# Gated two-branch decode attention in fp32: units of one head against units of four heads in three 8 MB tiles

## The chip, the core and the metric

The kernel runs on one core of one Trainium2 chip. The metric is the device time of one execution, in microseconds, smaller is better. The core has a matrix engine (PE, "TensorE") that multiplies from SBUF into PSUM, a vector engine (DVE), a scalar engine (ACT), GpSimd (POOL), a sync engine (SP) that here only issues transfers, and 16 DMA engines that carry every transfer between HBM and SBUF.

## What is computed

One decode step for two batch rows. Two attention branches A and B read the same `x`, each with its own query weights, key cache, value cache and output weights; a sigmoid gate mixes them. Everything is fp32.

```python
B, Sq, D = 2, 1, 512;  Hq, Sk, Dh = 32, 4096, 128
q = (x @ wq).reshape(B, Sq, Hq, Dh).transpose(0, 2, 1, 3)
scores = einsum("bhqd,bhkd->bhqk", q, k_cache) * Dh ** -0.5
o = einsum("bhqk,bhkd->bhqd", softmax(scores, axis=-1), v_cache)
branch = o.transpose(0, 2, 1, 3).reshape(B, Sq, Hq * Dh) @ wo
g = sigmoid((x * gate_w).sum(-1, keepdims=True))
out = g * branch_A + (1 - g) * branch_B
```

Each key or value cache is 2 x 32 heads x 4096 tokens x 128 floats, 134 MB, and there are four of them; each of the four weight matrices is 8 MB. Every byte is read once, 570 MB in all, and there is one query per head, so a byte of a cache is used for one multiply and one add.

## The kernel before

**Units.** The work is cut into 128 units, one head of one batch row of one branch each (`units`, L44), in the order branch, head, batch row. The 4096 tokens of a head lie on 128 partitions, 32 tokens to a partition, so a unit's K tile and its V tile are 128 x 4096 floats, 2 MB each, and a partition receives one run of 16 KB. There are four K buffers and five V buffers.

**A unit on the engines.** DVE multiplies the K tile in place by the query, which lies on all partitions (L141), sums over the 128 dimensions (L145), and takes the largest score per partition (L147). PE transposes that column (L151), DVE takes the maximum over partitions (L155), and ACT exponentiates, writing the weights into a zero-padded tile of 32 columns and the sums into `lp` (L158). PE multiplies the weights with V in eight matmuls, each of them in one of four strips of 32 array columns (L165); ACT copies the result to SBUF (L169); PE gathers one head's output (L177) and the sum of the exponentials over partitions (L184). DVE inverts that sum and normalises (L188, L192), and PE adds the head's share of the output projection (L197).

**What sets the order.** The schedule is manual: each engine executes its instructions in the order of the code. The main loop (L228) is a software pipeline: in the round of unit u it computes the scores of u, the softmax of u - 1 and the values of u - 2, and it normalises the pair of heads that is finished with u - 3. So DVE's `invert` and `normalise` stand one round or more behind the PE work that they read.

**Loads.** One list, `todo` (L208), sets the order of all loads on SP's queue: K two units ahead of V, a 2 MB piece of the query weights for each group of eight heads (`load_wq`, L69), and 1 MB of output weights for every four heads (`load_wo`, L75). SP waits at a load until the buffer it writes is free, and everything behind it in the list waits too. The small loads of `x` and of the gate weights come first (L82, L83). The query weights of the next group are projected between the units (`project`, L109), and the queries are copied from PSUM to SBUF by ACT (L119).

**The end.** The last V tile comes in four pieces (L65); after the last of them there follow the rest of that unit's values matmuls, ACT's copy, the gather, the normalisation, the output projection, the gated sum (L203) and the store (L205).

Of the kernel before, what the change touches and what calls it, by code (L numbers as in the profile page):

```python
# [13 lines left out]
P = 128  # L14
B = 2
# [4 lines left out]
NS = SK // P  # L20
KC = D // P
HG = 8
OG = 4
VC = 4
NVC = NS // VC
NPR = 3
QT = 32
STRIPS = P // QT
LEAD = 2
# [4 lines left out]
def tile_gated_decode(ctx: ExitStack, tc: tile.TileContext, ins: dict, out: bass.AP):  # L34
    nc = tc.nc
    consts = ctx.enter_context(tc.tile_pool(name="consts", bufs=1))
    kpool = ctx.enter_context(tc.tile_pool(name="kpool", bufs=4))
    vpool = ctx.enter_context(tc.tile_pool(name="vpool", bufs=5))
    wpool = ctx.enter_context(tc.tile_pool(name="wpool", bufs=2))
    work = ctx.enter_context(tc.tile_pool(name="work", bufs=3))  # L40
# [3 lines left out]
    units = [(n, h, b) for n in "AB" for h in range(H) for b in range(B)]  # L44
    NU = len(units)
    groups = [(n, g) for n in "AB" for g in range(H // HG)]
    per_group = HG * B

    kt, vt, wq, wo, qs = {}, {}, {}, {}, {}

    def tokens(cache, h, b):

        return cache[b, h].rearrange("(p r) d -> p r d", p=P)

    def load_k(u):
        n, h, b = units[u]
        kt[u] = kpool.tile([P, NS, DH], F32, name="kt")
        nc.sync.dma_start(kt[u], tokens(ins[n + "_k_cache"], h, b))

    def load_v(u):  # L60
        n, h, b = units[u]
        vt[u] = vpool.tile([P, NS, DH], F32, name="vt")
        src = tokens(ins[n + "_v_cache"], h, b)

        cuts = (0, NS) if u < NU - 1 else (0, NS // 2, 3 * NS // 4, NS - VC, NS)  # L65
        for i, j in zip(cuts, cuts[1:]):
            nc.sync.dma_start(vt[u][:, i:j], src[:, i:j])

    def load_wq(g):  # L69
        n, hg = groups[g]  # L70
        wq[g] = wpool.tile([P, KC, HG * DH], F32, name="wq", bufs=1)
        nc.sync.dma_start(
            wq[g], ins[n + "_wq"].rearrange("(c p) f -> p c f", p=P)[:, :, hg * HG * DH:(hg + 1) * HG * DH])

    def load_wo(n, hg):  # L75
        wo[n, hg] = wpool.tile([P, OG, D], F32, name="wo", bufs=2)
        nc.sync.dma_start(
            wo[n, hg], ins[n + "_wo"].rearrange("(h p) e -> p h e", p=P)[:, hg * OG:(hg + 1) * OG, :])


    rows = consts.tile([B * KC + KC, P], F32)
    nc.sync.dma_start(rows[:B * KC], ins["A_x"].rearrange("b s (c p) -> (b s c) p", p=P))  # L82
    nc.scalar.dma_start(rows[B * KC:], ins["gate_w"].rearrange("(c p) -> c p", p=P))  # L83
    load_wq(0)
# [4 lines left out]
    ones = consts.tile([P, P], F32)  # L89
    nc.vector.memset(ones, 1.0)  # L90


    padded = []
    for i in range(NPR):
        t = consts.tile([P, NVC, QT], F32, name=f"pr{i}")
        nc.vector.memset(t, 0.0)
        padded.append(t)

    pick = consts.tile([P, VC], F32)
    nc.vector.tensor_reduce(pick, ident.rearrange("p (s q) -> p q s", q=QT)[:, :VC, :], axis=AX.X, op=ALU.add)  # L100

    cols_ps = ps.tile([P, B * KC + KC], F32, name="mt", bufs=1)
    nc.tensor.transpose(cols_ps, rows, ident[:B * KC + KC, :B * KC + KC])
    cols = consts.tile([P, B * KC + KC], F32)
    nc.vector.tensor_copy(cols, cols_ps)
    xb = consts.tile([P, B * KC, P], F32)
    nc.vector.tensor_copy(xb, cols[:, :B * KC, None].to_broadcast([P, B * KC, P]))

    def project(g, i):  # L109

        b, half, c = i // (2 * KC), i // KC % 2, i % KC
        if i % (2 * KC) == 0:
            qs[g, b] = work.tile([P, HG * DH], F32, name=f"q{b}", bufs=2)
        if c == 0:
            qp[g] = ps.tile([P, HG * DH // 2], F32, name="qp", bufs=2)
        cols = slice(half * HG * DH // 2, (half + 1) * HG * DH // 2)
        nc.tensor.matmul(qp[g], xb[:, b * KC + c, :], wq[g][:, c, cols], start=c == 0, stop=c == KC - 1)  # L117
        if c == KC - 1:
            nc.scalar.activation(qs[g, b][:, cols], qp[g], AF.Copy, scale=SCALE)  # L119

    qp = {}
    for i in range(per_group):
        project(0, i)


    z = ps.tile([B, 1], F32, name="small", bufs=1)
    for c in range(KC):
        nc.tensor.matmul(z, cols[:, c:B * KC:KC], cols[:, B * KC + c:B * KC + c + 1],
                         start=c == 0, stop=c == KC - 1)
    gate = consts.tile([B, 4], F32)  # L130
    nc.scalar.activation(gate[:, 0:1], z, AF.Exp, scale=-1.0)  # L131
    nc.vector.tensor_scalar(gate[:, 1:2], gate[:, 0:1], 1.0, None, op0=ALU.add)  # L132
    nc.vector.reciprocal(gate[:, 2:3], gate[:, 1:2])
    nc.vector.tensor_scalar(gate[:, 3:4], gate[:, 2:3], -1.0, 1.0, op0=ALU.mult, op1=ALU.add)

    sc, rm, mt, pr, lp, vp, ot, ls, acc, part, vs, on, rs = ({} for _ in range(13))

    def scores_mult(u):
        n, h, b = units[u]
        q = qs[groups.index((n, h // HG)), b][:, (h % HG) * DH:(h % HG + 1) * DH]  # L140
        nc.vector.tensor_tensor(kt[u], kt[u], q[:, None, :].to_broadcast([P, NS, DH]), op=ALU.mult)  # L141

    def scores_sum(u):
        sc[u] = work.tile([P, NS], F32, name="sc")
        nc.vector.tensor_reduce(sc[u], kt[u], axis=AX.X, op=ALU.add)  # L145
        rm[u] = work.tile([P, 1], F32, name="rm")
        nc.vector.tensor_reduce(rm[u], sc[u], axis=AX.X, op=ALU.max)  # L147

    def spread_max(u):
        mt[u] = ps.tile([P, P], F32, name="mt", bufs=1)  # L150
        nc.tensor.transpose(mt[u], rm[u].to_broadcast([P, P]), ident)  # L151

    def soft(u):
        nm = work.tile([P, 1], F32, name="nm")
        nc.vector.tensor_reduce(nm, mt[u], axis=AX.X, op=ALU.max, negate=True)  # L155
        pr[u] = padded[u % NPR]
        lp[u] = work.tile([P, 1], F32, name="lp", bufs=4)
        nc.scalar.activation(pr[u][:, :, :VC], sc[u].rearrange("p (c a) -> p c a", a=VC), AF.Exp,  # L158
                             bias=nm, accum_out=lp[u])

    def values(u):
        vp[u] = ps.tile([P, VC * DH], F32, name="vp", bufs=2)
        for c in range(NVC):
            s = c % STRIPS
            nc.tensor.matmul(vp[u][s * QT:(s + 1) * QT], pr[u][:, c, :],  # L165
                             vt[u][:, c * VC:(c + 1) * VC, :].rearrange("p a d -> p (a d)"),
                             start=c < STRIPS, stop=c >= NVC - STRIPS)
        vs[u] = work.tile([P, VC * DH], F32, name="vs", bufs=1)
        nc.scalar.activation(vs[u], vp[u], AF.Copy)  # L169

    def gather_out(u):
        n, h, b = units[u]
        if b == 0:
            ot[n, h] = ps.tile([P, B], F32, name="ot", bufs=1)
        o = ot[n, h]
        for a in range(VC):
            nc.tensor.matmul(o[:, b:b + 1], vs[u][:, a * DH:(a + 1) * DH], pick[:, a:a + 1],  # L177
                             start=a == 0, stop=a == VC - 1)

    def sum_of(u):  # L180
        n, h, b = units[u]
        if b == 0:
            ls[n, h] = ps.tile([P, B], F32, name="small", bufs=1)
        nc.tensor.matmul(ls[n, h][:, b:b + 1], ones, lp[u], start=True, stop=True)  # L184

    def invert(n, h):
        rs[n, h] = work.tile([P, B], F32, name="rs")
        nc.vector.reciprocal(rs[n, h], ls[n, h])  # L188

    def normalise(n, h):  # L190
        on[n, h] = work.tile([P, B], F32, name="on")
        nc.vector.tensor_tensor(on[n, h], ot[n, h], rs[n, h], op=ALU.mult)  # L192

    def project_out(n, h):
        if h == 0:
            acc[n] = ps.tile([B, D], F32, name="acc", bufs=1)
        nc.tensor.matmul(acc[n], on[n, h], wo[n, h // OG][:, h % OG, :], start=h == 0, stop=h == H - 1)  # L197
        if h == H - 1:
            part[n] = consts.tile([B, D], F32, name="part" + n)
            if n == "A":  # L200
                nc.vector.tensor_scalar(part[n], acc[n], gate[:, 2:3], None, op0=ALU.mult)  # L201
            else:
                nc.vector.scalar_tensor_tensor(part[n], acc[n], gate[:, 3:4], part["A"],  # L203
                                               op0=ALU.mult, op1=ALU.add)
                nc.sync.dma_start(out.rearrange("b s e -> (b s) e"), part[n])  # L205


    todo = []  # L208
    for u in range(-LEAD, NU):
# [3 lines left out]
        if u < 0:  # L213
            continue
# [63 lines left out]
```

## Time and profile before

| | |
|---|---|
| median of 3 runs | 1349.0 us (1348.57 to 1349.04) |
| the profiled execution's own span, first to last instruction | 1344.6 us |
| median less that span | 4.4 us |
| bytes read from HBM | 570.43 MB |
| mean granted TensorE clock | 0.714 |
| DVE busy / PE busy / ACT busy | 1181.0 / 819.0 / 149.0 us |
| K loads, V loads | 128 and 128 of 2 MB (the last V in four pieces) |

A page of the profile shows how long each engine was busy, the span in 40 equal slices, the DMA queues, the chain of work that ended last, and the groups of instructions. L141 is line 141 of the kernel. PE is busy with matmuls, PEld with weight loads; an fp32 matmul appears as two records. A queue's packets are its transfers' runs: a row of 16 KB that goes to one partition is one packet of one DMA engine. "Landing" is the moment at which a transfer's completion is seen.

### The profile page before, as it was taken

Reading aid. Unit: us, or ns where it says so; the run is one execution under the profiler, and the core shown is the slowest. Engines: PE = TensorE matmul, PEld = TensorE weight load, DVE = VectorE, ACT = ScalarE, POOL = GpSimd, SP = SyncE. Lnnn points to the kernel's source line nnn. Section 1 sums busy time; section 2 is a strip of 40 time slices with the busy share of each in tenths; the row PEclk is TensorE's granted clock in tenths of the full one; section 3 lists DMA queues with packets and bytes.
Section 4 is the critical chain, followed back from the end, with each engine's and each line's share of the span. In section 5 each row is a group of like instructions: output and inputs, shape, how many; then the busy total and the mean of one; then the engine's idle time right before and its main releaser. Section 6 shows DMA issues by size and latency. Waiting matters only on the chain.

```text
span 1344.6 us, 9688 instructions
## 1 busy us (share of the span) xinstructions
PE 819.0 (61%) x3849; PEld 326.5 (24%) x3849; DVE 1181.0 (88%) x652; ACT 149.0 (11%) x418; POOL 0.7 (0%) x6
## 2 busy tenths in 40 slices
PE   5468755657545675466754666557665466655566
PEld 2223322322212222122212223122222122222222
DVE  2999997989889898898988989889898898989985
ACT  1011110111100111011100111101110011110111
POOL 0000000000000000000000000000000000000000
PEclk9568776688666876678866678656786677866667
DMA  9999999999999999999999999999999999999996
GB/s 390 429 434 428 430 429 429 432 429 429 430 430 432 429 429 428 429 431 431 430 429 428 429 431 432 427 431 427 432 432 427 432 429 429 431 428 432 428 431 266
DMA packets 50041, 571.07 MB, mean 425 GB/s; under 512 B 4542, under 2 KB 4554, under 8 KB 17228
## 3 DMA queue, kind: packets, MB, share of 16 engines
q1 hardware_dynamic: 49988, 570.45, 99.6%
q8 instruction: 30, 0.49, 0.1%
q14 instruction: 15, 0.12, 0.0%
q10 hardware_dynamic: 8, 0.00, 0.0%
HBM read 570.43 MB, written 0.00 MB: 424 GB/s over the span
## 4 chain that ended last, share of the span: by engine, by line
DMA 68%; DVE 27%; PE 2%; issue 2%; ACT 0%; SPq 0%; ACTq 0%
DMA kt<-in_B_k_cache_dram 36%; DMA kt<-in_A_k_cache_dram 27%; DVE sc L145 14%; DVE kt L141 12%; DMA vt<-in_B_v_cache_dram 3%; DMA vt<-in_A_v_cache_dram 2%; PE qp L117 1%; PE vp L165 1%; DMA wq<-in_A_wq_dram 1%; PE acc L197 0%; DVE nm L155 0%; DVE rm L147 0%; PE ot L177 0%; DVE on L192 0%; DVE partA L201 0%
## 5 line engine op out<-in xcount | busy, mean ns | idle before, releaser
L165 PE MATMUL vp<-vt,pr 128*32 128x512 f32 x2048 | 417.9, 961 | 422.1 <-DMA vt<-in_B_v_cache_dram 237.3
L141 DVE TENSOR_TENSOR kt<-kt,q 128x4096 f32<-128x4096 f32 x128 | 566.1, 4422 | 117.7 <-DMA kt<-in_B_k_cache_dram 65.1
L145 DVE TENSOR_REDUCE sc<-kt 128x32 f32<-128x4096 f32 x128 | 564.2, 4408 | 0.3 <-DVE nm L155 0.3
L165 PEld LDWEIGHTS vp<-vt,pr 128*32 128x32 f32 x2048 | 71.5, 147 | 578.9 <-DMA vt<-in_B_v_cache_dram 242.6
L177 PEld LDWEIGHTS ot<-pick,vs 128*128 128x128 f32 x1024 | 149.8, 223 | 13.9 <-issue 10.2
L177 PE MATMUL ot<-pick,vs 128*128 128x1 f32 x1024 | 141.2, 259 | 0.8 <-ACT vs L169 0.8
L117 PE MATMUL qp<-wq,xb 128*128 128x512 f32 x256 | 133.6, 651 | 6.3 <-DMA wq<-in_A_wq_dram 6.3
L169 ACT ACTIVATE vs<-vp 128x512 f32<-128x512 f32 x128 | 76.3, 596 | 443.8 <-PE vp L165 443.8
L158 ACT ACTIVATE pr<-sc,nm 128x32 f32<-128x32 f32 x128 | 41.1, 321 | 688.4 <-DVE nm L155 688.4
L151 PE MATMUL mt<-ident,rm 128*128 128x128 f32 x128 | 44.2, 345 | 90.8 <-DVE rm L147 90.6
L197 PE MATMUL acc<-wo,on 128*2 128x512 f32 x128 | 95.6, 841 | 0.3 <-DVE on L192 0.3
L117 PEld LDWEIGHTS qp<-wq,xb 128*128 128x128 f32 x256 | 48.3, 208 | 112.2 <-issue 112.2
L151 PEld LDWEIGHTS mt<-ident,rm 128*128 128x128 f32 x128 | 18.7, 146 | 222.5 <-DVE rm L147 193.5
L184 PE MATMUL small<-lp,ones 128*128 128x1 f32 x256 | 51.5, 271 | 0.0
L184 PEld LDWEIGHTS small<-lp,ones 128*128 128x128 f32 x256 | 45.3, 221 | 0.0
L155 DVE TENSOR_REDUCE nm<-mt 128x1 f32<-128x128 f32 x128 | 36.2, 283 | 0.3 <-PE mt L151 0.3
L197 PEld LDWEIGHTS acc<-wo,on 128*2 128x2 f32 x128 | 15.4, 122 | 83.7 <-issue 75.4
L147 DVE TENSOR_REDUCE rm<-sc 128x1 f32<-128x32 f32 x128 | 23.8, 186 | 4.4
L119 ACT ACTIVATE q<-qp 128x512 f32<-128x512 f32 x32 | 19.1, 597 | 56.8 <-PE qp L117 56.8
L158 ACT ACTIVATION_READ_ACCUMULATOR pr<-sc,nm 128x1 f32 x128 | 23.9, 187 | 0.0
L132 DVE TENSOR_SCALAR gate<-gate 2x1 f32<-2x1 f32 x1 | 0.1, 142 | 22.9 <-ACT gate L131 22.9
L188 DVE RECIPROCAL rs<-small 128x2 f32<-128x2 f32 x64 | 10.2, 160 | 5.6 <-PE small L184 5.6
(22 smaller groups left out, 16.6 us busy)
## 6 DMA issues: line engine op xcount, KB each, us to landing
kt<-in_A_k_cache_dram SPq DMA_DIRECT2D x64, 2048.0 KB, 30.0
vt<-in_A_v_cache_dram SPq DMA_DIRECT2D x64, 2048.0 KB, 34.4
kt<-in_B_k_cache_dram SPq DMA_DIRECT2D x64, 2048.0 KB, 32.4
vt<-in_B_v_cache_dram SPq DMA_DIRECT2D x63, 2048.0 KB, 35.5
wq<-in_A_wq_dram SPq DMA_DIRECT2D x4, 2048.0 KB, 14.4
wo<-in_A_wo_dram SPq DMA_DIRECT2D x8, 1024.0 KB, 31.9
wq<-in_B_wq_dram SPq DMA_DIRECT2D x4, 2048.0 KB, 34.0
wo<-in_B_wo_dram SPq DMA_DIRECT2D x8, 1024.0 KB, 32.0
```

Source lines behind the costliest of these rows:

```text
L117: nc.tensor.matmul(qp[g], xb[:, b * KC + c, :], wq[g][:, c, cols], start=c == 0, stop=c == KC - 1)
L141: nc.vector.tensor_tensor(kt[u], kt[u], q[:, None, :].to_broadcast([P, NS, DH]), op=ALU.mult)
L145: nc.vector.tensor_reduce(sc[u], kt[u], axis=AX.X, op=ALU.add)
L147: nc.vector.tensor_reduce(rm[u], sc[u], axis=AX.X, op=ALU.max)
L151: nc.tensor.transpose(mt[u], rm[u].to_broadcast([P, P]), ident)
L155: nc.vector.tensor_reduce(nm, mt[u], axis=AX.X, op=ALU.max, negate=True)
L158: nc.scalar.activation(pr[u][:, :, :VC], sc[u].rearrange("p (c a) -> p c a", a=VC), AF.Exp, bias=nm, accum_out=lp[u])
L165: nc.tensor.matmul(vp[u][s * QT:(s + 1) * QT], pr[u][:, c, :], vt[u][:, c * VC:(c + 1) * VC, :].rearrange("p a d -> p (a d)"), start=c < S ...
L169: nc.scalar.activation(vs[u], vp[u], AF.Copy)
L177: nc.tensor.matmul(o[:, b:b + 1], vs[u][:, a * DH:(a + 1) * DH], pick[:, a:a + 1], start=a == 0, stop=a == VC - 1)
L184: nc.tensor.matmul(ls[n, h][:, b:b + 1], ones, lp[u], start=True, stop=True)
L197: nc.tensor.matmul(acc[n], on[n, h], wo[n, h // OG][:, h % OG, :], start=h == 0, stop=h == H - 1)
```

## The change

**Units of four heads.** A unit is now four heads of one batch row (`HU` = 4), 32 units in the order branch, batch row, group of four heads. Each head takes 32 partitions and a partition holds 128 tokens (`SLOTS`). A K or V tile is 128 x 16384 floats, 8 MB, and a partition receives one run of 64 KB. A pad of 96 floats in front brings the tiles' SBUF addresses to multiples of 512 bytes. There are two buffers named `kt` and one named `vt`, and nothing else of that size: the query weights of a branch (8 MB in one load) and B's output weights take a `kt` buffer, A's output weights the `vt` buffer, and the last V tile a `kt` buffer.

**Scores.** The multiply reads the query from PSUM: the projection of a branch writes four PSUM tiles `q`, in strips, where the 32 partitions of each head hold that head's query, and they stay there. The maximum per head is found by a 32 x 32 transpose on DVE and no longer by PE. Four exponentials per unit, one for each head's 32 partitions, write one padded tile `pr`, and their sums go into a column per head of `lsum`.

**Values.** 32 matmuls per unit; an even and the following odd unit add into one PSUM tile, which ACT copies after the odd one; one matmul with `strip` puts the pair into its 32 rows of `gat`. After the last group of a batch row (`g == HG - 1`, units 7, 15, 23 and 31) `outputs` picks, sums, normalises and gates the 32 heads at once.

**No software pipeline.** The loop does scores, softmax and values of the same unit in one round; `outputs` stands in the round of its last unit. The loads stand in the loop: after softmax u comes the load of K u + 2, after values u that of V u + 1. In rounds 14 and 15 B's query weights and the first two K tiles of B come in.

**Output weights last.** Both branches' output weights are loaded after the last V tile, B's in six pieces, and the whole output projection follows the loop. The gate is applied in `outputs`, so that A and B add into one PSUM tile.

**Small loads.** `x` and the gate weights now come in three loads on ACT's queue, 128 rows of 16 bytes each. SP's first load is A's query weights. `z`, the gate's sum, is one matmul that stands on PE ahead of the projection and needs all three of them.

```diff
-    units = [(n, h, b) for n in "AB" for h in range(H) for b in range(B)]
+    units = [(n, b, g) for n in "AB" for b in range(B) for g in range(HG)]
...
+    def cache(name, u):
+        n, b, g = units[u]
+        c = ins[f"{n}_{name}_cache"][b, g * HU:(g + 1) * HU]
+        return c.rearrange("h (s t) d -> (h s) t d", t=SLOTS)
...
+    def load_wq(n):
+        wq[n] = big.tile([P, KC, H * DH], F32, name="kt")
+        nc.sync.dma_start(wq[n], ins[n + "_wq"].rearrange("(p c) f -> p c f", c=KC))
...
+    load_wq("A")
+    xg = consts.tile([P, B + 1, KC], F32)
+    for b in range(B):
+        nc.scalar.dma_start(xg[:, b], ins["A_x"][b, 0].rearrange("(p c) -> p c", c=KC))
+    nc.scalar.dma_start(xg[:, B], ins["gate_w"].rearrange("(p c) -> p c", c=KC))
+    load_k(0)
...
+    z = ps.tile([H, B], F32, name="small")
+    nc.tensor.matmul(z, ones, zp, start=True, stop=True)
...
+    def project(n):
+        for b in range(B):
+            for half in range(2):
+                q = ps.tile([P, HG // 2, DH], F32, name="q", bufs=4)
...
+                for c in range(KC):
+                    for h in range(HU):
+                        nc.tensor.matmul(
+                            q[h * QP:(h + 1) * QP], xb[:, b, c, :],
+                            cols[:, c, h, half * HG // 2:(half + 1) * HG // 2, :],
+                            start=c == 0, stop=c == KC - 1)
...
+    def scores(u):
+        n, b, g = units[u]
+        q = qs[n, b, g // (HG // 2)][:, g % (HG // 2), :]
+        nc.vector.tensor_tensor(kt[u], kt[u], q[:, None, :].to_broadcast([P, SLOTS, DH]), op=ALU.mult)
+        sc[u] = work.tile([P, SLOTS], F32, name="sc")
+        nc.vector.tensor_reduce(sc[u], kt[u], axis=AX.X, op=ALU.add)
...
+        if odd:
+            vs = work.tile([P, VC * DH], F32, name="vs", bufs=1)
+            nc.scalar.activation(vs, o, AF.Copy)
...
+            nc.tensor.matmul(gat[n, b][r:r + QP], strip, vs, start=True, stop=True)
+            if g == HG - 1:
+                outputs(n, b)
+
+    def outputs(n, b):
+        gs = work.tile([P, VC, DH], F32, name="vs", bufs=1)
+        nc.scalar.activation(gs, gat[n, b].rearrange("p (a d) -> p a d", a=VC), AF.Copy)
+        lt = ps.tile([H, 1], F32, name="small")
+        nc.tensor.matmul(lt, lsum, ones[:, 0:1], start=True, stop=True)
+        rl = work.tile([H, 2], F32, name="rl")
+        nc.vector.reciprocal(rl[:, 0:1], lt)
+        nc.vector.tensor_tensor(rl[:, 1:2], rl[:, 0:1], gate[:, 2 + (n == "B"), b:b + 1], op=ALU.mult)
...
+    project("A")
+    load_k(1)
+    load_v(0)
+    for u in range(NU):
+        scores(u)
+        soft(u)
+        if u == per_branch - 2:
+            load_wq("B")
+        elif u == NU - 2:
+            load_v(NU - 1)
+        elif u == NU - 1:
+            load_wo("B")
+        else:
+            load_k(u + 2 if u != per_branch - 1 else per_branch)
+            if u == per_branch - 1:
+                project("B")
+                load_k(per_branch + 1)
+        values(u)
+        if u == NU - 2:
+            load_wo("A")
+        elif u < NU - 2:
+            load_v(u + 1)
```

Three places where the order of instructions differs. First DVE in the middle of a branch, before: `kt` is a K tile, `small` the PSUM tile of the sums, `rs` its reciprocal, `ot` and `on` a head's output.

```order
L145 TENSOR_REDUCE sc_1386<-kt_1270 128x32
L147 TENSOR_REDUCE rm_1388<-sc_1386 128x1
L188 RECIPROCAL rs_1402<-small_1356 128x2
L141 TENSOR_TENSOR kt_1306<-kt_1306,q0_995 128x4096
L155 TENSOR_REDUCE nm_1415<-mt_1404 128x1
L192 TENSOR_TENSOR on_1419<-ot_1372,rs_1402 128x2
L145 TENSOR_REDUCE sc_1421<-kt_1306 128x32
```

And DVE now, from the scores of unit 7, the last of its batch row, to those of unit 8: `rl` is the reciprocal of the sums `small`.

```order
L147 TENSOR_TENSOR kt_452<-kt_452,q_129 128x16384
L149 TENSOR_REDUCE sc_542<-kt_452 128x128
L154 TENSOR_REDUCE rm_544<-sc_542 128x1
L156 STREAM_TRANSPOSE tm_546<-rm_544 128x32
L158 TENSOR_REDUCE nm_548<-tm_546 128x1
L193 RECIPROCAL rl_595<-small_593 32x1
L194 TENSOR_TENSOR rl_595<-rl_595,gate_107 32x1
L147 TENSOR_TENSOR kt_504<-kt_504,q_146 128x16384
```

The reciprocal before read the sums of a unit that PE had in an earlier round; now it reads the sums of the unit that DVE has just scored, and the multiply of the next unit stands behind it.

Next the first instructions of SP's queue, before (`rows` is the tile of `x`):

```order
L82 DMA rows<-in_A_x_dram 8x128
L72 DMA wq<-in_A_wq_dram 128x4x1024
L58 DMA kt<-in_A_k_cache_dram 128x4096 x3
L77 DMA wo<-in_A_wo_dram 128x4x512
L67 DMA vt<-in_A_v_cache_dram 128x4096
```

and now, where `kt` is the buffer that holds the query weights, then K tiles:

```order
L72 DMA kt<-in_A_wq_dram 128x16384
L61 DMA kt<-in_A_k_cache_dram 128x16384 x2
L68 DMA vt<-in_A_v_cache_dram 128x16384
L61 DMA kt<-in_A_k_cache_dram 128x16384
L68 DMA vt<-in_A_v_cache_dram 128x16384
```

`x` is gone from SP's queue, and the second K tile goes into the buffer of the query weights. Last the start of ACT's queue now; `xg` holds `x` and the gate weights:

```order
L87 DMA xg<-in_A_x_dram 128x4 x2
L88 DMA xg<-in_gate_w_dram 128x4
L121 ACT_TABLE_LOAD
L121 ACTIVATE gate<-small 32x2
L162 ACTIVATE pr,lsum<-sc,nm 32x32x4 x8
```

Before there was one load there, the gate weights in four rows of 512 bytes.

More of the change, by code (lines that the diff above doesn't have):

```diff
@@ L186, in invert @@
[L186 to L205, printed above, removed]
```

275 lines of the change are left out of this document (120 added, 155 removed).

## The prediction

> **What bounds the kernel now.** I read the page first: the slices, then the chain.
>
> ```profile
> span 1344.6 us, 9688 instructions
> ...
> PE 819.0 (61%) x3849; PEld 326.5 (24%) x3849; DVE 1181.0 (88%) x652; ACT 149.0 (11%) x418; POOL 0.7 (0%) x6
> ...
> GB/s 390 429 434 428 430 429 429 432 429 429 430 430 432 429 429 428 429 431 431 430 429 428 429 431 432 427 431 427 432 432 427 432 429 429 431 428 432 428 431 266
> ...
> HBM read 570.43 MB, written 0.00 MB: 424 GB/s over the span
> ...
> DMA 68%; DVE 27%; PE 2%; issue 2%; ACT 0%; SPq 0%; ACTq 0%
> ```
>
> The row of GB/s is flat from the second slice to the last but one, the chain is mostly K loads, and no engine is busy all the time (DVE 88%). So the transfers set the time. The stretch between the ends, and two stretches of it with the runs sorted by size, say how fast they go (the last columns of the first row are granted clock, DMA share, GB/s):
>
> ```profile
> 20.00:1320.00 1300.00, 792.00 (x3739) 314.92 (x3738) 1168.41 (x635) 143.86 (x408) 0.00 (x0) 0.71 1.01 430
> ```
>
> ```profile
> DMA packets 1249, 18.12 MB, mean 431 GB/s; under 512 B 143, under 2 KB 143, under 8 KB 143
> ```
>
> ```profile
> DMA packets 463, 1.89 MB, mean 421 GB/s; under 512 B 1, under 2 KB 1, under 8 KB 463
> ```
>
> The first stretch moves 430 GB/s, and 570.43 MB at that rate are 1326.6 us of a span of 1344.6 us. The second (62 to 104 us) holds K and V runs of 16 KB only, the third (44.9 to 49.4 us) the query weights' runs of 4 KB. Only three things can change the time: the rate, holes in the stream of transfers, and what lies ahead of the first and behind the last.
>
> **Rate.** At 431 GB/s a run of 16 KB takes one of 16 DMA engines 16384 x 16 / 431 = 608 ns; at 421 one of 4 KB takes 155.7 ns. The difference, 452 ns for 12288 bytes, is 36.8 ns per KB of 1000 bytes; what is left of a run is 4.9 ns of its own. A 64 KB run comes to 4.9 + 2413 = 2418 ns, or 433.7 GB/s. Nothing of before moves a 64 KB run, so the bounds are 430 (no gain) and 434; I take 433, near the extrapolation, since nearly all bytes now come in such runs. 570.43 / 0.433 = 1317.4 us, 9.2 us less than now; at 430 it is 1326.6, at 434 1314.4. An 8 MB tile takes 19.4 us.
>
> One rule speaks against the longer runs. The Trainium skill, DMA: Bandwidth & Descriptors, section Latency and other measured facts, lists transfers whose 128 rows lie a large power of two apart in HBM: 207 GB/s at 512 KiB against 214 at full rate, 164 at 2 MiB. Here the pitch goes from 16 to 64 KiB, which it does not list, and no run here shows it; if the 3% of 512 KiB held, an estimate by that page is 41 us more. I give it no more than 2 in 100.
>
> **Compute beside it.** These rows carry the price of a unit of four heads:
>
> ```profile
> L141 DVE TENSOR_TENSOR kt<-kt,q 128x4096 f32<-128x4096 f32 x128 | 566.1, 4422 | 117.7 <-DMA kt<-in_B_k_cache_dram 65.1
> L145 DVE TENSOR_REDUCE sc<-kt 128x32 f32<-128x4096 f32 x128 | 564.2, 4408 | 0.3 <-DVE nm L155 0.3
> ...
> L155 DVE TENSOR_REDUCE nm<-mt 128x1 f32<-128x128 f32 x128 | 36.2, 283 | 0.3 <-PE mt L151 0.3
> ...
> L147 DVE TENSOR_REDUCE rm<-sc 128x1 f32<-128x32 f32 x128 | 23.8, 186 | 4.4
> ```
>
> The multiply and the sum over a tile four times as large cost at most 4 x 4422 = 17.7 us each; if up to 186 ns of each (the 32-element row L147) is a fixed part, at least 17.1. I take 17.25, so 34.5 us for both. That the multiply now reads its query from PSUM I price at nothing (L155 reads 128 elements from PSUM in 283 ns, L147 32 from SBUF in 186: 1 ns per element either way); 0.5 us a unit is the other bound. With the small maximum steps (under 1 us) DVE needs about 35.4 us per unit, the transfers 38.7. So DVE stays under cover, by 3 us per unit. For PE:
>
> ```profile
> 8.93 16.80 PE L117 MATMUL qp<-wq,xb 128*128 128x512 f32 x32 [6.28 <-DMA wq<-in_A_wq_dram]
> ...
> 14.18 0.34 PEld L117 LDWEIGHTS qp<-wq,xb 128*128 128x128 f32 x1 [0.52 <-issue]
> 14.84 0.19 PEld L117 LDWEIGHTS qp<-wq,xb 128*128 128x128 f32 x1 [0.32 <-issue]
> ...
> 45.71 3.42 PE L165 MATMUL vp<-vt,pr 128*32 128x512 f32 x16
> ```
>
> The first row is a dense burst that starts cold: the weight loads take 0.34 us until 14.18 and 0.19 us from 14.84 on, when the clock doubles, some 5.6 us after the start. The last row is one unit's eight strip matmuls at half clock, 0.43 us each. At the end of the span they run at full clock:
>
> ```profile
> 1336.57 1.92 PE L165 MATMUL vp<-vt,pr 128*32 128x512 f32 x16
> ...
> 1337.02 0.13 PEld L165 LDWEIGHTS vp<-vt,pr 128*32 128x32 f32 x4 [0.30 <-issue]
> 1337.45 0.13 PEld L165 LDWEIGHTS vp<-vt,pr 128*32 128x32 f32 x4 [0.30 <-issue]
> 1338.67 0.60 ACT L169 ACTIVATE vs<-vp 128x512 f32<-128x512 f32 x1 [4.39 <-PE vp L165]
> ...
> 1339.32 1.05 PE L177 MATMUL ot<-pick,vs 128*128 128x1 f32 x8 [0.83 <-ACT vs L169]
> 1340.41 0.16 DVE L192 TENSOR_TENSOR on<-ot,rs 128x2 f32<-128x2 f32 x1 [3.57 <-PE ot L177]
> ...
> 1341.68 0.74 DVE L203 SCALAR_TENSOR_TENSOR partB<-acc,gate,partA 2x512 f32<-2x512 f32 x1 [1.11 <-PE acc L197]
> 1342.45 0.27 SPq L205 DMA_DIRECT2D out_dram<-partB  x1
> ```
>
> Four weight loads (two matmuls) per 0.43 us are 0.215 us per matmul. The 32 values matmuls of a unit follow over 25 us of idle PE: 5.6 us cold (13 of them), 19 warm at 0.215, with the last one's drain 9.9 us. The 64 projection matmuls by the same account take 16.7 us. The bounds are 7.7 to 13.7 and 15 to 27 us (all warm, all cold). V u + 1 may load only when values u is done, with one V buffer: 9.9 us fit into the 19.4 us that K u + 2 loads meanwhile. In most rounds nothing stops the stream.
>
> **Hole 1, in the rounds of units 7 and 23.** The reciprocal in `outputs` (L193 of the changed kernel) stands on DVE ahead of the multiply of unit 8, and it waits for PE's values of unit 7. Behind DVE waits SP: the load of K 10 needs the buffer of K 8. Count from the landing of V 7, the time at which DVE has long scored unit 7 (its tile landed three transfers, 58 us, earlier). Values: 9.9 us. Then ACT's copy, the gather matmul, the sums and two DVE operations; in the rows above the same way from the last values matmul (1338.49) by ACT and PE to DVE (1340.41) takes 1.9 us, and a 512-column matmul of up to 0.9 us takes the place of the gather: 2.6 us. Scores of unit 8: 34.5, handoffs 0.2. Then K 10 is issued. From issue to flowing data costs a transfer
>
> ```profile
> DMA to landing us min/median/max: 7.6/33.3/35.0
> ```
>
> at most 7.6 - 4.9 = 2.7 us (the first query weights, 2 MB, 4.9 us of bytes); part of that is receipt that a full stream hides, so 2.0. Until then the queue holds K 9 and V 8, 38.75 us. The hole is 9.9 + 2.6 + 34.5 + 0.2 + 2.0 - 38.75 = 10.4 us. The same holds for unit 23; 20.8 us together (16 to 30 by the bounds of PE and DVE). After unit 15 the next K comes late anyhow, behind the query weights, and unit 31 has no scores behind it.
>
> **Hole 2, at the start.** K 1 goes into the buffer of A's query weights, so it waits for the whole projection, and PE's `z` ahead of it waits for three small loads on ACT's queue.
>
> ```profile
> 0.73 0.55 ACTq L83 DMA_DIRECT2D rows<-in_gate_w_dram  x1
> ...
> 0.74 0.39 SPq L82 DMA_DIRECT2D rows<-in_A_x_dram  x1
> ```
>
> SP's first load, now the query weights, goes out at 0.74 us and lands at 0.74 + 2.7 + 19.4 = 22.8, K 0 at 42.2. ACT's loads take about 0.55 us each to issue, so the second and third get to the DMA engines when the first 64 KB runs already move. Each has 8 rows and a completion on every engine, 18 packets, and a packet is not cut into by another queue's:
>
> ```profile
> q8 instruction: 1, 0.02, 4.9%
> ```
>
> In this window of 1.2 us one 16 KB packet of instructions took 4.9% of 16 engines, 0.94 us, longer than the 608 ns it costs alone, so its queue and SP's take turns at the engine and don't run at once. If each small packet waits its turn behind one 64 KB run of 2.4 us, the 16 runs of the weights and K 0 all pass first, and the last small row lands with K 0, at 42.2. Then three small DVE steps and `z` (1.2 us), the projection (16.7) and K 1's issue (2.0): a hole of 19.9 us. The Trainium skill, same page, section Queues, rings and completion order, says that an engine goes round its queues packet by packet and drains a whole packet of typically 9 to 17 descriptors before it switches. By that rule the third load still comes after K 0, so its sum is the one below; without turns it is the first rival's. No run here has a small load among big ones that could show it.
>
> **Ends.** First landing overhead 0.74 + 2.7 = 3.4 us. Behind the last landing there are now a few 128-column matmuls (about 0.5), a copy (0.2) and the store: in the rows above the gated sum ended at 1342.42 and the span at 1344.6, 2.2 us, with a second store per queue 2.5. That is 3.2 us; now 8.0 us pass from the last values burst (1336.57) to the end.
>
> **Sum.** 3.4 + 1317.4 + 19.9 + 20.8 + 3.2 = 1364.7 us of span; with the 4.4 us by which the median of the runs exceeds the profiled span, 1369 us. 0.2%, 2.7 us, is about what a measurement of this kernel can tell from no change.
>
> **The rivals.** *The small loads slip through* (ends on the other side, no change): the 16-byte rows get between the big runs at once and land before the query weights, by 22.8 us. The projection ends at 39.6, before K 0, and hole 2 is gone: 1369 - 19.9 = 1349 us. It decides at a landing of `x` and gate weights by about 25 us. For it: the rows are tiny and the first load may be through before the weights' first run. Its range is 1342 (434 GB/s, small holes) to 1359 (430). *The long runs are cut*: if a 64 KB row travels as four packets of 16 KB, a turn lasts 0.61 us, 18 turns 11 us, so no hole 2, but also no gain of rate: 1349 + 9.2 = 1358 us. *Turns cost extra*: the instruction packet took 0.33 us more than its bytes; 36 changes of queue at that price add 12 us: 1381 us. *PE stays at half clock*: each hole 1 grows by 3.8 us, the projection by 10.7, and B's projection delays a load by up to 7: about 1394 us; against it speaks that dense bursts in the rows above did warm up.
>
> **How the numbers follow.** Forecast 0.38, small loads slip through 0.35, cut runs 0.10, costly turns 0.10, half clock 0.07. The forecast's own range is 1361 to 1378 (rate and holes). The range for all, 1344 to 1385, leaves out the fast end of the first rival (0.09) and most of half clock (0.07). Faster by over 0.2%: 0.14 of the first rival and 0.01 of cut runs, 0.15. Within 0.2%: 0.12 and 0.02, 0.14. Slower: the rest, 0.71.
>
> **What would show it.** Right: the slices show GB/s low in the second slice (34 to 67 us) and in the two slices around 400 to 420 and 1060 to 1080 us and flat elsewhere; SP's load of K 1 goes out near 60 us, when the projection (L136) ends; DVE waits for PE's sums at L193 some 35 us in each of three rounds; `xg` lands after 40 us. Wrong: `xg` lands by 25 us; a mean rate between holes under 430 or over 435 GB/s; packets of under 64 KB; no wait at L193; or a V load that waits for values in every round, which I hold to be covered.

## The result and the profile after

| | before | after |
|---|---|---|
| median of 4 runs | 1348.78 us (1346.54 to 1349.04) | 1368.64 us (1366.86 to 1369.55) |
| ratio to before, 95% interval | | 1.0158 (1.0141 to 1.0175) |
| span of the profiled execution | 1344.6 us | 1365.1 us |

The kernel is 20 us slower, and the forecast was 1369 us. The page of the changed kernel:

```profile
span 1365.1 us, 5925 instructions
...
PE 358.5 (26%) x2578; PEld 100.0 (7%) x2578; DVE 1127.3 (83%) x184; ACT 82.1 (6%) x283; POOL 1.8 (0%) x8
...
GB/s 411 204 430 430 431 430 431 430 437 444 434 408 307 442 444 433 430 430 431 434 431 436 433 436 431 430 436 438 433 430 432 306 430 429 430 434 431 444 438 349
...
q1 hardware_dynamic: 10520, 570.43, 96.8%
...
q10 hardware_dynamic: 440, 0.01, 0.0%
...
L147 DVE TENSOR_TENSOR kt<-kt,q 128x16384 f32<-128x16384 f32 x32 | 550.9, 17215 | 43.1 <-DMA kt<-in_A_k_cache_dram 23.0
L149 DVE TENSOR_REDUCE sc<-kt 128x128 f32<-128x16384 f32 x32 | 551.0, 17220 | 3.2
```

The row of GB/s is no longer flat: slice 2, slices 12 and 13, and slice 32 (of 34 us each) are low, the places named beforehand. The windows of the same trace, three in these slices and three between them (the last columns are granted clock, DMA share and GB/s):

```profile
41.60:59.10 17.50, 15.39 (x130) 5.38 (x130) 12.07 (x7) 0.16 (x1) 0.00 (x0) 1.00 0.01 1
409.00:418.70 9.70, 0.00 (x0) 0.00 (x0) 9.60 (x4) 0.00 (x0) 0.00 (x0) 0.50 0.00 0
1058.90:1068.30 9.40, 0.00 (x0) 0.00 (x0) 9.30 (x5) 0.04 (x1) 0.00 (x0) 0.50 0.00 0
66.00:400.00 334.00, 78.28 (x530) 21.33 (x530) 279.70 (x42) 19.96 (x70) 0.00 (x0) 0.61 1.00 433
430.00:1050.00 620.00, 162.42 (x1132) 45.28 (x1132) 532.60 (x81) 37.95 (x132) 0.00 (x0) 0.63 1.00 433
1080.00:1340.00 260.00, 68.36 (x474) 19.55 (x474) 234.79 (x40) 17.94 (x62) 0.00 (x0) 0.64 1.00 432
```

The transfers stand still three times, and between the holes they run at 432 to 433 GB/s, where before had 430. These windows count a packet where it starts, so a short one is off by up to a run at its edges, and the 16 DMA engines do not run dry at the same moment: around unit 7 the first does at 408.5 us and the last at 410.1. By the start and the end of each packet in the trace, an engine stands idle for 18.0, 10.2 and 9.9 us in the mean, 38.1 together. The longer runs win back some 9 (570.43 MB at 433 GB/s in place of 430), and the two ends of the span some 8: the first slice has 411 GB/s for 390 before, the last 349 for 266. DVE takes 17.22 us for each pass over a tile.

The timeline of the first hole (start, duration, engine; in brackets the idle time before and what ended it):

```profile
0.73 0.90 ACTq L87 DMA_DIRECT2D xg<-in_A_x_dram  x2
0.73 0.40 SPq L72 DMA_DIRECT2D kt<-in_A_wq_dram  x1
...
1.19 57.45 SPq L61 DMA_DIRECT2D kt<-in_A_k_cache_dram  x2
...
1.67 0.45 ACTq L88 DMA_DIRECT2D xg<-in_gate_w_dram  x1
...
42.23 0.29 DVE L112 TENSOR_SCALAR xb<-xg 128x256 f32<-128x256 f32 x1 [39.56 <-DMA xg<-in_A_x_dram]
...
42.86 1.08 PE L136 MATMUL q<-kt,xb 128*32 128x512 f32 x3
...
42.98 15.26 PE L136 MATMUL q<-kt,xb 128*32 128x512 f32 x125
```

The 2 KB of `x` are issued at 0.73 us and are there at 42.23, when all 16 MB of the query weights and of K 0 have passed. The row of L61 spans both K loads: the second ends at 1.19 + 57.45 = 58.64, right after the projection (42.98 + 15.26 = 58.24). The second hole, around unit 7:

```profile
371.93 9.48 PE L174 MATMUL vp<-vt,pr 128*32 128x512 f32 x64 [28.60 <-DMA vt<-in_A_v_cache_dram]
...
383.25 0.15 DVE L193 RECIPROCAL rl<-small 32x1 f32<-32x1 f32 x1 [33.99 <-PE gat L183]
...
383.51 17.20 DVE L147 TENSOR_TENSOR kt<-kt,q 128x16384 f32<-128x16384 f32 x1
...
400.82 17.22 DVE L149 TENSOR_REDUCE sc<-kt 128x128 f32<-128x16384 f32 x1
418.06 0.33 SPq L61 DMA_DIRECT2D kt<-in_A_k_cache_dram  x1
```

V 7 lands at 371.93; values, small steps and the two passes of unit 8 follow one upon another until K 10 goes out at 418.06; by then all DMA engines have been idle since 410.1. Among the waits (us in all, times, the longest):

```profile
DVE rl L193 <- PE gat L183: 113.2, 4, 34.0
```

```profile
SPq L68 <- PE vp L174: 278.5, 30, 11.5
```

The first is the reciprocal's: 34.0 and 33.9 us in units 7 and 23, 31.6 in unit 15, which makes no hole, and 13.7 in the last unit. The second says that 30 V loads wait for values, 9 us each, and it costs nothing: the window from 66 to 400 us has a DMA share of 1.00, since K loads fill the time. A wait of a queue is a loss only where nothing else is in flight.

### The profile page after: what moved, and what is told of

Read it like the earlier page. It is cut to its first block, busy times and chain, and to the rows that moved or that the text cites. A ratio compares the mean times of both kernels' runs of the same rounds, so it can differ in the third digit from the quotient of the medians.

```text
span 1365.1 us, 5925 instructions
## 1 busy us (share of the span) xinstructions
PE 358.5 (26%) x2578; PEld 100.0 (7%) x2578; DVE 1127.3 (83%) x184; ACT 82.1 (6%) x283; POOL 1.8 (0%) x8
## 3 DMA queue, kind: packets, MB, share of 16 engines
q1 hardware_dynamic: 10520, 570.43, 96.8%
HBM read 570.43 MB, written 0.00 MB: 418 GB/s over the span
## 4 chain that ended last, share of the span: by engine, by line
DMA 57%; DVE 21%; PE 17%; another core or an unknown queue 3%; issue 0%; ACT 0%; SPq 0%; ACTq 0%; DVEq 0%
DMA vt<-in_A_v_cache_dram 33%; PE vp L174 16%; DMA vt<-in_B_v_cache_dram 15%; DVE sc L149 10%; DVE kt L147 10%; DMA xg<-in_A_x_dram 3%; DMA kt<-in_B_wo_dram 3%; DMA kt<-in_B_k_cache_dram 3%; PE q L136 1%; PE gat L183 0%; ACT pr L162 0%; DVE rm L154 0%; ACT vs L179 0%; SPq L82 0%
## 5 line engine op out<-in xcount | busy, mean ns | idle before, releaser
L147 DVE TENSOR_TENSOR kt<-kt,q 128x16384 f32<-128x16384 f32 x32 | 550.9, 17215 | 43.1 <-DMA kt<-in_A_k_cache_dram 23.0
L149 DVE TENSOR_REDUCE sc<-kt 128x128 f32<-128x16384 f32 x32 | 551.0, 17220 | 3.2
L174 PE MATMUL vp<-vt,pr 128*32 128x512 f32 x1984 | 278.6, 725 | 916.3 <-DMA vt<-in_A_v_cache_dram 422.8
L162 ACT ACTIVATE pr<-sc,nm 32x128 f32<-32x128 f32 x128 | 66.4, 519 | 837.8 <-DVE nm L158 835.1
L193 DVE RECIPROCAL rl<-small 32x1 f32<-32x1 f32 x4 | 0.6, 156 | 113.2 <-PE gat L183 113.2
L136 PE MATMUL q<-kt,xb 128*32 128x512 f32 x256 | 31.3, 650 | 10.8 <-DMA kt<-in_B_wq_dram 10.8
L179 ACT ACTIVATE vs<-vp 128x512 f32<-128x512 f32 x16 | 9.6, 597 | 365.0 <-PE vp L174 365.0
L162 ACT ACTIVATION_READ_ACCUMULATOR pr<-sc,nm 32x1 f32 x128 | 25.4, 198 | 0.0
L183 PE MATMUL gat<-vs,strip 128*32 128x512 f32 x32 | 16.7, 604 | 11.4 <-ACT vs L179 11.4
L136 PEld LDWEIGHTS q<-kt,xb 128*32 128x32 f32 x256 | 9.5, 119 | 31.7 <-issue 20.0
L154 DVE TENSOR_REDUCE rm<-sc 128x1 f32<-128x128 f32 x32 | 9.2, 286 | 1.1
## 6 DMA issues: line engine op xcount, KB each, us to landing
kt<-in_B_wo_dram SPq DMA_DIRECT2D x2, 256.0 KB, 40.5
```

The source lines that it names most:

```text
L136: nc.tensor.matmul(q[h * QP:(h + 1) * QP], xb[:, b, c, :], cols[:, c, h, half * HG // 2:(half + 1) * HG // 2, :], start=c == 0, stop=c == ...
L154: nc.vector.tensor_reduce(rm[:, 0:1], sc[u], axis=AX.X, op=ALU.max)
L162: nc.scalar.activation(w, sc[u][r].rearrange("p (c a) -> p c a", a=VC), AF.Exp, bias=nm[r], accum_out=lsum[r, g * HU + h:g * HU + h + 1])
L174: nc.tensor.matmul(o[s * QP:(s + 1) * QP], pr[:, c, at:at + QP], vt[u][:, c * VC:(c + 1) * VC, :].rearrange("p a d -> p (a d)"), start=not ...
L179: nc.scalar.activation(vs, o, AF.Copy)
L183: nc.tensor.matmul(gat[n, b][r:r + QP], strip, vs, start=True, stop=True)
```

## The experiments

The theory: two independent mechanisms, each with its own holes. At the start the 16-byte rows of `x` and of the gate weights take turns with whole 64 KB runs, one row to a run; in units 7 and 23 the reciprocal holds up the multiply of the next unit and so a K load. The rivals: what else stands in those places (the buffer that K 1 shares, the work on 32 heads), or the tiles' form (alignment, length of the runs). Before ran beside each of the three groups of experiments, with medians of 1346.5, 1346.8 and 1348.1 us; each ratio is to these.

**Each mechanism alone, and both.** The start first: the three small loads on SP's queue, ahead of the query weights.

```diff
-    load_wq("A")
...
-        nc.scalar.dma_start(xg[:, b], ins["A_x"][b, 0].rearrange("(p c) -> p c", c=KC))
-    nc.scalar.dma_start(xg[:, B], ins["gate_w"].rearrange("(p c) -> p c", c=KC))
+        nc.sync.dma_start(xg[:, b], ins["A_x"][b, 0].rearrange("(p c) -> p c", c=KC))
+    nc.sync.dma_start(xg[:, B], ins["gate_w"].rearrange("(p c) -> p c", c=KC))
+    load_wq("A")
```

> The changed kernel with one edit: the three small loads of x and the gate weights are issued on SP's queue ahead of the query weights. Theory (they wait their turns behind 64 KB runs, and K 1 waits for the projection behind them): xg lands by about 4 us instead of 42, the projection ends near 39 us, the hole at the start (17.9 us in the changed kernel's trace) is gone, SP's first big load goes out 1.2 us later: about 1368.6 - 17 = 1352 us. Rival (128 rows of 16 bytes are slow by themselves, or hold up the big runs wherever they stand): the query weights land late by what the small loads took, gain under 5 us, 1364 us or more. Both leave the holes after units 7 and 23 at about 9.6 us each.

Measured: 1350.45 us, ratio 1.0028 (1.0014 to 1.0041). Its timeline:

```profile
2.60 38.43 SPq L61 DMA_DIRECT2D kt<-in_A_k_cache_dram  x2
2.96 0.29 DVE L112 TENSOR_SCALAR xb<-xg 128x256 f32<-128x256 f32 x1 [0.29 <-DMA xg<-in_A_x_dram]
...
24.09 16.54 PE L136 MATMUL q<-kt,xb 128*32 128x512 f32 x128 [20.07 <-DMA kt<-in_A_wq_dram]
```

`x` is there at 2.96, the projection now waits for its weights and ends at 40.6, and K 1 goes out before K 0 has landed. The start hole is gone, though K 1 still shares the buffer of the query weights; the two later ones stay. Next the other mechanism: `outputs` one round later, behind the scores of the next unit.

```diff
-            if g == HG - 1:
-                outputs(n, b)
...
+        if u and units[u - 1][2] == HG - 1:
+            outputs(*units[u - 1][:2])
...
+    outputs("B", B - 1)
```

> The changed kernel with one edit: outputs of a batch row stands after the scores of the next unit, no longer ahead of them, so that DVE's reciprocal no longer holds up the multiply of units 8 and 24. Theory (that wait makes the holes): DVE's waits at the reciprocal vanish, both holes of about 9.6 us go, the start stays: about 1368.6 - 19 = 1349 us. Rival (the holes come from one V buffer: the load of V 8 and K 10 would wait for PE's values anyway): the holes stay or move to the V load, gain under 4 us, 1365 us or more.

Measured: 1347.92 us, ratio 1.0012 (1.0003 to 1.0021). The slices of its page, with DVE's group at the reciprocal (now L191):

```profile
GB/s 405 199 424 436 435 436 435 434 431 432 432 425 436 437 436 433 432 434 433 435 437 422 433 428 433 432 435 428 430 435 436 435 434 435 434 437 434 430 435 334
```

```profile
L191 DVE RECIPROCAL rl<-small 32x1 f32<-32x1 f32 x4 | 0.6, 148 | 14.8 <-PE gat L183 14.8
```

Only slice 2 is low; of the wait of 113.2 us there are left 14.8, all at the end of the last unit, where no scores follow. Both edits together:

> Both edits of the two runs before: small loads first on SP, and outputs after the next unit's scores. Theory (three holes, independent of each other): 1368.6 - 17 - 19 = 1332 us, GB/s flat from the second slice to the last but one, faster than both kernels. Rival (a stream without holes runs into the next limit, DVE with 35.2 us per unit and late loads, or engines of the DMA that drift apart): new holes of some us in several rounds, 1340 us or more.

Measured: 1330.33 us, ratio 0.9880 (0.9865 to 0.9896), faster than both kernels. From 1.0158 the ratio falls by 0.0130 through the first edit, by 0.0146 through the second, and by 0.0278 through both: the mechanisms add. The middle of its trace, without a hole (the DMA share is 1.00):

```profile
34.00:1290.00 1256.00, 361.48 (x2272) 96.49 (x2268) 1123.53 (x167) 78.18 (x277) 0.00 (x0) 0.60 1.00 433
```

**How the small loads wait.** Here V 0 is loaded ahead of K 1, so that the queue doesn't run dry after K 0.

```diff
-    load_k(1)
     load_v(0)
+    load_k(1)
```

> The changed kernel with one edit: V 0 is loaded ahead of K 1; the small loads stay on ACT's queue. Theory (the hole is there because K 1 stands ahead of V 0 in SP's queue and waits for the projection): xg still lands at about 42 us, but V 0 fills the stream until about 61 us while the projection ends at about 58; the hole goes, 1368.6 - 18 = 1351 us. Rival (late small loads cost by delaying scores 0 and so DVE for good): K 2 then waits for DVE instead and the gain is under 5 us, 1364 us or more.

Measured: 1372.53 us, ratio 1.0195 (1.0175 to 1.0214). The theory's time failed, and the rival's was met. The timeline shows why:

```profile
42.55 0.29 DVE L112 TENSOR_SCALAR xb<-xg 128x256 f32<-128x256 f32 x1 [39.89 <-DMA xg<-in_A_x_dram]
61.88 0.17 DVE L114 TENSOR_TENSOR xw<-xg 128x8 f32<-128x8 f32 x1 [19.04 <-DMA xg<-in_gate_w_dram]
...
78.47 0.33 SPq L61 DMA_DIRECT2D kt<-in_A_k_cache_dram  x1
```

`x` lands as before, but the gate weights, the third load, only with the end of V 0, so the projection starts at 62.3 and the hole has moved there. The rival's mechanism has a share too: K 2 now waits for DVE's late scores of unit 0, and around 102 us the engines stand idle for another 4.4 us. For the gate weights, then, 18 turns are not enough. The packets of the two queues over 16 engines, first in this run from 4.5 to 60 us, then in the changed kernel from 4.5 to 41 us and, last, from 40.5 to 43 us:

```profile
q1 hardware_dynamic: 400, 24.12, 100.5%
q10 hardware_dynamic: 400, 0.01, 0.4%
```

```profile
q1 hardware_dynamic: 256, 15.73, 99.5%
q10 hardware_dynamic: 256, 0.00, 0.4%
```

```profile
q10 hardware_dynamic: 176, 0.00, 4.0%
q1 hardware_dynamic: 16, 0.00, 0.4%
```

SP's queue is q1, ACT's q10. As many small packets pass as packets of SP's queue, one for one: 256 to 256 and 400 to 400. 15.73 MB are 240 runs of 65536 bytes, 15 to an engine, and 16 completions. All three loads need 3 x (8 rows + 1 completion) = 27 turns per engine. In the changed kernel 16 of them go by until 41 us, and the last 11 (176 packets) at once when SP's queue has run dry. With V 0 behind K 0 the queue doesn't run dry, and 25 turns last until V 0 ends. Next, shorter turns in the changed kernel: A's query weights in four loads, with runs of 16 KB.

```diff
-        nc.sync.dma_start(wq[n], ins[n + "_wq"].rearrange("(p c) f -> p c f", c=KC))
+        src = ins[n + "_wq"].rearrange("(p c) f -> p c f", c=KC)
+        for c in range(KC if n == "A" else 1):
+            part = slice(c, c + 1) if n == "A" else slice(0, KC)
+            nc.sync.dma_start(wq[n][:, part], src[:, part])
```

> The changed kernel with one edit: A's query weights are loaded in four pieces, so in runs of 16 KB; the small loads stay on ACT's queue, K and V keep their 64 KB runs. Theory (a small packet waits for one run of the other queue, whatever its length): a turn costs about 0.7 us, the 27 small packets of an engine (three loads of 8 rows and a completion) pass in some 19 us, xg lands by about 21 us, before the weights, and the hole at the start goes: about 1351 us. Rival (the small loads wait until SP's queue runs dry, however it is cut): xg lands at about 42 us as before and the time stays at 1368 us.

Measured: 1349.40 us, ratio 1.0020 (1.0011 to 1.0029). Its timeline, and its packets from 4 to 16 us:

```profile
13.13 0.29 DVE L115 TENSOR_SCALAR xb<-xg 128x256 f32<-128x256 f32 x1 [10.46 <-DMA xg<-in_A_x_dram]
18.11 0.17 DVE L117 TENSOR_TENSOR xw<-xg 128x8 f32<-128x8 f32 x1 [4.69 <-DMA xg<-in_gate_w_dram]
```

```profile
q1 hardware_dynamic: 336, 4.98, 97.3%
q10 hardware_dynamic: 336, 0.00, 1.6%
```

One for one again, 21 turns per engine in 12 us, 0.57 us each. The small loads are in by 18.1 us, and the start hole is gone: a turn costs what the other queue's packet takes. Last, V 0 ahead of K 1 with only `x` left on ACT's queue and the gate weights first on SP's.

```diff
+    nc.sync.dma_start(xg[:, B], ins["gate_w"].rearrange("(p c) -> p c", c=KC))
     load_wq("A")
...
-    nc.scalar.dma_start(xg[:, B], ins["gate_w"].rearrange("(p c) -> p c", c=KC))
...
-    load_k(1)
     load_v(0)
+    load_k(1)
```

> V 0 ahead of K 1 as in the run that gained nothing, and the gate weights alone moved to SP's queue ahead of the query weights; x stays on ACT's queue. Theory (each small packet takes one turn of 2.5 us; 27 turns outlasted V 0 there, 18 remain here): xg lands at about 46 us, the projection ends near 62, about when V 0 does, and K 1 leaves a hole of 2 to 4 us instead of 18: about 1354 us. Rival (small rows come through only when SP's queue is dry): xg lands at about 62 us as in that run, 1370 us or more.

Measured: 1350.62 us, ratio 1.0028 (1.0017 to 1.0040). `x` came sooner than either side said:

```profile
1.19 0.42 SPq L72 DMA_DIRECT2D kt<-in_A_wq_dram  x1
...
23.49 0.29 DVE L112 TENSOR_SCALAR xb<-xg 128x256 f32<-128x256 f32 x1 [20.82 <-DMA xg<-in_A_x_dram]
```

```profile
q10 hardware_dynamic: 144, 0.00, 2.5%
```

The weights' load goes out 0.45 us later, behind the gate weights, and until 3.0 us (the last row) 144 small packets of ACT's queue are through: 9 per engine, the whole first load. They pass from 1.8 to 2.2 us; the first long runs start at 2.2, in the changed kernel at 1.8. Nine turns are left and pass by 23.5 us. There is no start hole, which is why the time comes near the theory's though the landing does not. So the slipping ahead that the prediction gave to the first load happens, but hangs on when the weights' first runs come, here by 0.45 us; in the changed kernel it did not happen. No run delays the weights without putting small packets ahead of them on SP's queue, so that the time alone does it is not shown.

**The wait of DVE, put in four times more.** After units 3, 11, 19 and 27 DVE copies a sum that PE takes behind the values; nobody uses the copy.

```diff
+            elif g == HG // 2 - 1:
+                lt = ps.tile([H, 1], F32, name="small")
+                nc.tensor.matmul(lt, lsum, ones[:, 0:1], start=True, stop=True)
+                rl = work.tile([H, 2], F32, name="rl")
+                nc.vector.tensor_copy(rl[:, 0:1], lt)
```

> The changed kernel with the same kind of wait put in at four more places: after the values of units 3, 11, 19 and 27 (the middle of each batch row) PE sums the exponentials seen so far, and DVE copies that sum, whose result nobody uses, ahead of the next unit's multiply. Nothing else differs. Theory (a wait of DVE for the values of the unit it has just scored costs the same anywhere in a stream that has one V buffer: values, small steps and scores follow one upon another, 48.6 us against 38.8 us of queued transfers): four more holes in the transfers, of 9.5 to 9.9 us as in units 7 and 23, so 1368.6 + 39 = about 1408 us (1400 to 1412), and DVE waits some 34 us at the copy four times. Rival (the holes of units 7 and 23 come from what else stands in those rounds: ACT's copy of the 32 heads, the gating and the picks on PE): the copy waits but K loads go on almost unbroken, under 1 to 2 us each, 1370 to 1377 us.

Measured: 1411.54 us, ratio 1.0476 (1.0458 to 1.0493): 42.9 us more than the changed kernel. Its slices, the group of the copy, and the stretch behind the start:

```profile
GB/s 417 209 417 447 417 445 434 313 418 445 436 370 357 423 439 436 311 429 434 445 421 428 431 432 433 432 317 419 444 421 417 311 432 438 428 326 419 443 421 359
...
L190 DVE COPY rl<-small 32x1 f32<-32x1 f32 x4 | 0.6, 146 | 106.6 <-PE gat L183 58.9
```

```profile
62.00:1350.00 1288.00, 310.85 (x2148) 84.17 (x2152) 1087.57 (x167) 76.59 (x269) 0.00 (x0) 0.62 0.96 412
```

Four new low slices (8, 17, 27 and 36) beside the old ones. 412 GB/s against 433 over 1288 us are 62.5 us lost to six holes, 10.4 each. The work on 32 heads has no part in it; one short instruction of DVE at the wrong place is enough. DVE's waits did not come as expected: 106.6 us in four, a mean of 27 and not 34. The hole is as large as elsewhere all the same, since it is counted from the landing of V to the next K's issue, and where DVE had stood before that doesn't enter.

**The tiles' form.** Both kernels are the one with both edits, with one thing changed. First the pad, so that the tiles start 256 bytes off a multiple of 512:

```diff
-PAD = 96
+PAD = 32
```

> The kernel with both fixes (small loads first, outputs late; 1330.3 us) with a pad of 32 floats instead of 96: the three big tiles then begin 256 bytes off a multiple of 512, as the tiles of the kernel before do. Theory (a run has a small fixed cost, paid once per 64 KB; where it begins in SBUF plays no part): a 64 KB run stays at 2418 ns, time within 2 us of 1330.3. Rival (the gain of rate comes from the alignment): a run takes at least 1% longer, 1343 us or more.

Measured: 1330.80 us, ratio 0.9878 (0.9865 to 0.9892); without the shift 0.9880. The shift of 256 bytes plays no part. Then the K and V loads in four loads each, with runs of 16 KB as in the kernel before (V in the same way):

```diff
-        nc.sync.dma_start(kt[u], cache("k", u))
+        for i in range(0, SLOTS, SLOTS // 4):
+            nc.sync.dma_start(kt[u][:, i:i + SLOTS // 4], cache("k", u)[:, i:i + SLOTS // 4])
```

> The kernel with both fixes (1330.3 us) with every K and V load cut into four loads of a quarter of the slots each, so in runs of 16 KB; the weights keep their 64 KB runs. Theory (4.9 ns of its own per run, and three more completions per load and engine at 9 ns): a run of 16 KB takes 608 to 611 ns, four of them 14 to 26 ns more than one of 64 KB, in all 8 to 16 us more: 1338 to 1346 us. Rival (the rate is set elsewhere, by the port or by engines drifting apart): no difference, 1330 to 1333 us.

Measured: 1336.91 us, ratio 0.9928 (0.9915 to 0.9942), 6.6 us more than with long runs, a little below the theory's figures and well above the rival's. The middle of its trace:

```profile
34.00:1290.00 1256.00, 387.87 (x2244) 81.64 (x2236) 1124.49 (x167) 77.36 (x273) 0.00 (x0) 0.63 1.01 431
```

431 against 433 GB/s: 570.43 MB at these rates differ by 6.1 us. Four runs for one also mean four completions for one; the two prices are not separated.

## Why the prediction was right

*Rate.* 433 GB/s was taken and 432 to 433 measured between the holes; the runs go as whole (240 in 15.73 MB). The stream as a whole took 1365.1 - 38.1 - 3.3 - 3.4 = 1320.3 us, 2.9 more than the 1317.4 of the sum (3.3 for the start: the query weights are issued at 0.73 us and land 21.9 later, of which the eight runs of 2.418 on each engine are 19.3). The rate was used for all bytes, but after a standstill every engine's first run is slow. At the start, from 0 to 4.5 us, there are

```profile
q1 hardware_dynamic: 16, 1.05, 69.2%
```

16 runs, one on each engine, of 69.2% of 4.5 us, 3.1 us each, where most runs take 2.42; after the three holes it is 3.1, 3.0 and 3.0 us. Those three make 1.8 us of the 2.9. The rest was not traced.

*Hole 1.* 10.4 us were forecast, 10.2 and 9.9 measured, with two errors against each other. From V 7's landing to K 10's bytes it took 47.3 us, not 49.2: values 9.5 for 9.9, small steps 2.1 for 2.6, scores 34.5 as said, and from issue to flow 1.2 (418.06 to 419.2, in the mean of the engines) for 2.0. And the engines had only 37.2 us of K 9 and V 8 left, not 38.75, since V 7's landing is seen 1.6 us after its last bytes. The extra waits and the later `outputs` show the mechanism from both sides. Unit 15's wait makes no hole, as was said: slices 17 to 24 lie at 430 to 436. And a V load waits for values in nearly every round, which the forecast held to be covered: it is.

One reading of the kernel before has to be put right. Its `sum_of` and `invert` of a pair of heads stand in the same round, not a round apart. But that sum is of a unit scored two rounds earlier and stands on PE ahead of the round's values, and DVE waited for it 5.6 us in all (L188 <- PE small L184). What matters is not the round but whether the operand hangs on the newest transfer.

*Hole 2.* 19.9 forecast, 18.0 measured. The engines run dry at 41.4 us in the mean, 0.8 before `x` is seen, where the forecast began to count. From there it took 17.2 us: 0.6 to the projection for 1.2, the projection 15.4 for 16.7, and 1.2 from its end to K 1's bytes for 2.0. That the small loads wait for the end of K 0 was right, and 42.2 was the moment. The count behind it failed: "the second and third get to the DMA engines when the first 64 KB runs already move" left the first load out, which gave 18 turns, just the 16 runs of the weights and of K 0 and two completions. In fact all 27 queue, 16 pass, and the other 11 get through because SP's queue is dry. Both counts give the same moment here, and V 0 ahead of K 1 tells them apart: by 18 turns it would have cured the hole, by 27 it only moves it, and it moved.

The rule that an engine drains a whole packet, typically 9 to 17 descriptors, before it switches (the Trainium skill, DMA: Bandwidth & Descriptors, section Queues, rings and completion order) does not fit this trace. From 14 to 24 us there are

```profile
q1 hardware_dynamic: 80, 4.19, 96.8%
q10 hardware_dynamic: 80, 0.00, 0.5%
```

five small packets and five of SP's queue on each engine, singly; a load's nine in one piece would give none or nine. The same section's round robin between the queues agrees with the equal counts.

*Ends.* Behind the last landing 3.2 us were forecast; the timeline has 1365.1 - 1361.73 = 3.4:

```profile
1361.73 0.40 PE L247 MATMUL q<-kt,on 128*2 128x128 f32 x8 [0.24 <-DMA kt<-in_B_wo_dram]
...
1362.19 0.29 DVE L250 COPY res<-q 128x128 f32<-128x128 f32 x1 [24.72 <-PE q L247]
1362.51 0.64 SPq L254 DMA_DIRECT2D out_dram<-res  x2
```

*Sum.* 3.3 + 1320.3 + 18.0 + 20.1 + 3.4 = 1365.1 us of span against 1364.7: +2.9 of the stream, -1.9 and -0.7 of the holes, -0.1 and +0.2 of the ends nearly cancel. The median lies 3.5 above that span, where 4.4 were taken. The closeness is partly luck; the holes' places and causes are not.

*The rivals.* The small loads did not slip through, the long runs were not cut, and PE warmed up (granted clock 1.00 in the start hole). Turns cost next to nothing: from the end of the first run on an engine (5.09 us in the mean) to the end of its sixteenth (41.43) pass 36.34 us, and 15 runs of 2.418 are 36.27, so the turns beside them add under 0.1 us and not 12. The row pitch, for which the list in the Trainium skill (DMA: Bandwidth & Descriptors, section Latency and other measured facts) has 3% at 512 KiB, cost nothing measurable at 64 KiB: 433 GB/s. Its 2 in 100 stood outside the five chances, which add up to 1 without it.

## What to carry to other kernels

Where one big buffer of each kind is all that fits, ask of each instruction on the engine that frees buffers whether its operand hangs on the newest transfer; if so, put it behind the next unit's work. Small loads that the first compute needs go ahead of the big ones on the same queue, since on another queue each of their rows may wait for a whole run. And price a stall from the landing to the next issue, less what is still queued: neither the wait of an engine (34 us here, for a hole of 10) nor that of a queue (30 V loads of 9 us, for none) is its cost.

## What the runs showed of the hardware

- A row of 16 bytes on ACT's queue and a 64 KB run on SP's pass one for one on each DMA engine: the two loads of `x`, 2 KB each, needed 41.5 us (0.73 to 42.23), against 2.2 us (0.74 to 2.96) ahead of the big loads on SP's queue. With 16 KB runs beside it, a turn takes 0.57 us.
- With the big load issued 0.45 us later, behind a small one on its own queue, the first small load on the other queue got ahead of it: `x` was there at 23.5 us in place of 42.2 or 42.6.
- After a standstill the first 64 KB run on each DMA engine took 3.0 to 3.1 us, and most others 2.42.
- 64 KB runs are worth 0.5% over 16 KB runs in four loads for one (1330.3 against 1336.9 us), and 256 bytes of shift of the tiles in SBUF nothing (1330.8).
